# Inverses of chunks one and two in rounds of two batches, with the early parts and the first feed-forward steps dealt out anew

## The chip, the cores and the metric

The kernel runs on one core of one Trainium2 chip. The metric is the device time of one execution in microseconds (us). Every input lies in HBM before the launch, and the output is written back to HBM.

## What is computed

The reference is a recurrent attention block (RWKV-7) followed by a feed-forward block (FFN) with a squared ReLU, all in float32:

```python
# batch 4, heads 8, sequence 768, head size 40; state starts at zero
for t in range(S):
    y[:, :, t] = einsum('bhd,bhde->bhe', rt, state)
    Sa = einsum('bhde,bhe->bhd', state, at)
    state = state * wt[:, :, None, :] - einsum('bhd,bhe->bhde', Sa, bt)
    state = state + einsum('bhd,bhe->bhde', vt, kt)
# y as tokens: 3072 x 320
h = maximum(x @ w_in, 0)        # 320 -> 2048
out = (h * h) @ w_out           # 2048 -> 320
```

## The kernel before

The sequence is cut into six chunks of 128 positions. An **item** is one chunk of one batch; there are 24 items, numbered so that item `i` is chunk `i // 4` of batch `i % 4` (`order`, line 126). Inside a chunk the recurrence is solved with matrix products, for which the inverse of two triangular 64x64 blocks for each head is needed. The work of one item has these parts:

- `early(i)` (line 308, driven by `prepare`, line 623, which first loads the inputs of item `i + 1`): transposes of w, b and a on TensorE, cumulative products and reciprocals on VectorE, 16 products that give the triangular blocks `N`, a copy of them by ScalarE, and stores to HBM: the decays (`kept_e`), the triangular blocks (`kept_d`) and the block between the halves (`kept_n`). Stores are put into a list (`line`, line 86) and issued on SP's queue one or two ticks later; `flush` issues all that are left.
- `solve(u)` (line 360): one **round** of inverses, for a unit `u` of several items, on GpSimd (POOL). It loads the triangular blocks of the whole unit into `half_n`, clears `half_t`, and then goes through the 63 rows of a 64x64 block; for each row one multiplication (line 385) and one subtraction (line 387). Each block lies on several partitions, each of which holds a part of its columns: column `j` lies on class `j` modulo the number of classes. At the end the result is stored to `kept_t`.
- `rest(i)` (line 438): the part of an item that needs no state: it loads `dec` from `kept_e`, multiplies k and v and masks the products. It ends in `inverses(i)` (line 394), which loads `T` from `kept_t` on SP's queue. For the first item of a unit this load stands at the end of `rest`, for the others earlier.
- `chain(i)` (line 500): the part that needs the state and `T`. It is a chain of small products and copies, and gives the tokens of the item.
- the FFN (`ffn`, line 571): for each group of two items 16 steps that multiply by `w_in`, and then 8 steps that multiply by `w_out`, so 24 FFN steps for each of 12 groups. It starts on a group when both of its items are done.

A main loop (line 693) runs 24 steps. Step `i` runs `chain(i)`, `rest(i + 1)`, the early parts of some later items (`ahead`), a number of FFN steps (`share`; otherwise 12), and in steps 0 to 3 the rounding of the weights. `weave` (line 611) deals them out over 12 ticks, in program order for each engine. Each engine and each DMA queue works off its instructions in this order; an instruction that waits holds up what stands behind it on the same engine. SP's queue issues nearly all loads and stores; POOL's queue issues those of `solve`.

Units (line 272): chunk 0 is solved in two units of two batches with a finer scheme (`fine`), each of the chunks 1 to 5 in one unit of four batches, with each block's columns on two partitions (4 batches x 8 heads x 2 halves x 2 classes = 128 partitions). A unit of four items is solved after the step in which the early part of its fourth item is done: chunk 1 after step 1, chunk 2 after step 4, chunks 3 to 5 after steps 7, 11 and 15. Ahead of step 4 a stretch of its own runs 32 FFN steps together with the early parts of items 10 and 11 (`between`, line 686). No early part runs after step 15. After step 23 the rest of the FFN runs alone.

```python
        if u >= FINE:
            for col in range(2):
                queue.dma_start(out=T[col::2], in_=kept[col].rearrange("h f j t -> (f j) h t"))
```

Of the kernel before, what the change touches and what calls it, by code (L numbers as in the profile page):

```python
# [8 lines left out]
FP32 = mybir.dt.float32  # L9
# [8 lines left out]
def kernel(  # L18
# [22 lines left out]
    nc = tc.nc  # L41
# [64 lines left out]
    class Ring:  # L106
# [133 lines left out]
    def weights(n, pool=ps_f):  # L240
        for _ in range(n):
# [8 lines left out]
            else:  # L250
# [15 lines left out]
              for c in range(NCH)]  # L266
# [2 lines left out]
    kept_q = dram.tile([B, H, 2, 2, Q, Q], FP32, tag="q", name="kept_q")  # L269
    kept_m = [dram.tile([2, Q, H, Q], FP32, tag=f"m{i}", name=f"kept_m{i}") for i in range(B)]  # L270

    units = [(0, b0, 2) for b0 in range(0, B, 2)] + [(c, 0, B) for c in range(1, NCH)]
    FINE = B // 2
    unit_of = {c * B + b0 + n: u for u, (c, b0, nb) in enumerate(units) for n in range(nb)}
    kept_t = [dram.tile([2, nb, H, 2, 2, Q // 2, Q] if u < FINE else [2, nb, H, 2, Q, HC], FP32, tag=f"t{u}",
                        name=f"kept_t{u}") for u, (_, _, nb) in enumerate(units)]

    def turn(x_):
        p_ = psum(ps_w)
# [80 lines left out]
    def solve(u, queues):  # L360
        c, b0, nb = units[u]
        fine = u < FINE
        size = Q if fine else HC
        words = lambda t_, n: t_.rearrange("p s t -> p (s t)")[:, :n]
        if fine:
            parts = [words(new(f"half_n{u}", [128, Q, HC - u * Q], 1), Q * Q)]
            kept = [kept_q[b0:b0 + nb].rearrange("b h f k s t -> (b h f k) (s t)")]
            ts = words(solved, Q * HC)[:, u * Q * Q // 2:(u + 1) * Q * Q // 2]
        else:

            parts = [words(new(f"half_n{n}", [128, Q, HC - n * Q], 1), Q * (HC - n * Q)) for n in range(2)]
            kept = [k_.rearrange("b h f s t -> (b h f) (s t)") for k_ in kept_d[c]]
            ts = words(solved, Q * HC)
        for part, from_ in zip(parts, kept):
            for col in range(2):
                queues[col % len(queues)].dma_start(out=part[col * 64:(col + 1) * 64], in_=from_)  # L376
        nc.gpsimd.memset(ts, 0.0)
        for col in range(2):
            nc.gpsimd.memset(ts[col * 64:(col + 1) * 64, col::size + 2], -1.0)
        t3 = ts.rearrange("p (j t) -> p j t", t=size)  # L380
        for s in range(size - 1):
            n, m_ = s // 2 + 1, size - 1 - s
            row = parts[s // Q].rearrange("p (s t) -> p s t", s=Q)[:, s % Q, s % Q + 1:]
            p_ = new("half_p", [128, 528], 1)[:, :n * m_].rearrange("p (j t) -> p j t", j=n)
            nc.gpsimd.tensor_tensor(p_, row.unsqueeze(1).to_broadcast([128, n, m_]),  # L385
                                    t3[:, :n, s:s + 1].to_broadcast([128, n, m_]), Alu.mult)
            nc.gpsimd.tensor_tensor(t3[:, :n, s + 1:], t3[:, :n, s + 1:], p_, Alu.subtract)  # L387
        to = kept_t[u]
        to = to.rearrange("two b h f k j t -> (two b h f k) (j t)") if fine else to.rearrange("two b h f j t -> (two b h f) (j t)")
        nc.gpsimd.dma_start(out=to, in_=ts)  # L390
# [3 lines left out]
    def inverses(i, g, queue=nc.sync):  # L394
        bb, c = order[i]
        u = unit_of[i]
        kept = kept_t[u][:, bb - units[u][1]]
        g["T"] = T = new("T", [128, H, HC], 2)
        if u >= FINE:
            for col in range(2):  # L400
                queue.dma_start(out=T[col::2], in_=kept[col].rearrange("h f j t -> (f j) h t"))
        else:


            blocks = spare("blocks", i)
            for col in range(2):
                queue.dma_start(out=blocks[col::2], in_=kept[col].rearrange("h f k j t -> (f k j) h t"))
        if "N" not in g:
            g["N"] = new("N21", [HC, H, HC], 2)
            queue.dma_start(out=g["N"], in_=kept_n[i])  # L410
            if u < FINE:
                g["joins"] = spare("joins", i)
                for half in range(2):
# [209 lines left out]
    def prepare(i, g=None):  # L623
        if i + 1 < len(order) and i + 1 not in early_loaded:
            load_early(i + 1)
        yield from early(i, g)

    def some(gen, n):
        for _ in range(n):
            next(gen, None)  # L630
            yield
# [50 lines left out]


    TOTAL = STEPS // GB
    ahead = {0: (4, 5), 1: (6, 7), 2: (8,), 3: (9,)}
    between = {4: (10, 11)}
    ahead.update({i: (i + 8,) for i in range(4, len(order) - 8)})
    share = {0: (0, 0), 1: (0, 0), 2: (6, 0), 3: (6, 0), 4: (2, 32), 5: (2, 0)}
    rounded = {0: NARROW - WITH, 1: 5, 2: 5, 3: 6}
    rounding = weights(NARROW + NF)  # L690
    done = set(range(B))
    turn_of = B
    for i in range(len(order)):
        bb, c = order[i]
        n, before = share.get(i, (TOTAL, 0))
        if before:
            made = between.get(i, ())
            jobs = [(some(second, before), before, 0, before)]
            jobs += [(prepare(m_), 5, 8 * j, 8 * j + 10) for j, m_ in enumerate(made)]
            weave(*jobs)  # L700
            done.update(made)
        tc.no_sync_barrier()
        jobs = [(chain(i, ready.pop(i)), 9, 0, TOTAL)]
        if 1 < i + 1 < len(order):
# [8 lines left out]
        if i in rounded:  # L713
            jobs.append((some(rounding, rounded[i]), rounded[i], 0, TOTAL))
        weave(*jobs)
        if turn_of < len(order) and all(turn_of + n_ in done for n_ in range(B)):
            flush()
            solve(unit_of[turn_of], own)
            turn_of += B
    flush()  # L720
    run(second)
    flush()
# [29 lines left out]
```

## Time and profile before

| | us |
|---|---|
| median of 3 runs | 1226.81 |
| lowest and highest of them | 1225.35 and 1228.97 |
| the profiled execution | 1221.21 |
| span of the profiled execution, first to last instruction | 1219.5 |
| TensorE matmul busy | 1035.6 |
| VectorE busy | 491.8 |
| ScalarE busy | 243.5 |
| GpSimd busy | 623.5 |
| mean granted clock of TensorE | 0.878 |

The profile is one execution on the chip. Its page gives the busy time of each engine, the span in 40 slices of 30.5 us, the chain of work that ended last and the costliest groups of instructions. Of its trace one can ask for windows (the busy time of each engine in a stretch), the timeline of one engine, and groups of instructions by shape. In such rows `PE` is TensorE's products, `PEld` its weight loads, `DVE` VectorE, `ACT` ScalarE, `POOL` GpSimd; an engine's name with `q` is its queue or sequencer, so `SPq` shows the issues of DMAs by SP. Times are counted from the span's start. A bracket at the end of a timeline row is the idle time of the engine just before, and what ended it.

### The profile page before, as it was taken

Reading aid. Unit: us, or ns where it says so; the run is one execution under the profiler, and the core shown is the slowest. Engines: PE = TensorE matmul, PEld = TensorE weight load, DVE = VectorE, ACT = ScalarE, POOL = GpSimd, SP = SyncE. Lnnn points to the kernel's source line nnn. Section 1 sums busy time; section 2 is a strip of 40 time slices with the busy share of each in tenths; the row PEclk is TensorE's granted clock in tenths of the full one; section 3 lists DMA queues with packets and bytes.
Section 4 is the critical chain, followed back from the end, with each engine's and each line's share of the span. In section 5 each row is a group of like instructions: output and inputs, shape, how many; then the busy total and the mean of one; then the engine's idle time right before and its main releaser. Section 6 shows DMA issues by size and latency. Waiting matters only on the chain.

```text
span 1219.5 us, 18757 instructions
## 1 busy us (share of the span) xinstructions
PE 1035.6 (85%) x7504; PEld 857.1 (70%) x7504; DVE 491.8 (40%) x1012; ACT 243.5 (20%) x539; POOL 623.5 (51%) x846
## 2 busy tenths in 40 slices
PE   4347677787298989987999978999989999999998
PEld 3336566676177777776878766888768787888876
DVE  5384663566033245424335415435413242322311
ACT  1123212231021112121212121222122121221211
POOL 5670003999517998029996039995059993000000
PEclk9655565788689789997998997999989999999999
DMA  7954468260275643472553381554173113433000
GB/s 97 175 128 104 94 134 164 93 122 37 66 146 99 116 78 77 110 141 72 93 124 81 69 155 53 95 121 107 47 143 63 34 48 84 81 63 74 2 13 11
DMA packets 260822, 110.23 MB, mean 90 GB/s; under 512 B 242944, under 2 KB 248064, under 8 KB 259456
## 3 DMA queue, kind: packets, MB, share of 16 engines
q1 hardware_dynamic: 251824, 83.87, 35.4%
q0 software_dynamic: 2640, 14.16, 4.4%
q10 hardware_dynamic: 6272, 11.01, 3.3%
q8 instruction: 59, 0.97, 0.3%
q14 instruction: 27, 0.22, 0.1%
HBM read 73.28 MB, written 34.74 MB: 89 GB/s over the span
## 4 chain that ended last, share of the span: by engine, by line
PE 60%; POOL 9%; DVE 7%; DMA 5%; SPq 3%; issue 1%; ACT 0%; DVEq 0%; ACTq 0%; POOLq 0%
PE ps_f L77 34%; PE ps_c L77 16%; PE ps_w L77 6%; POOL half_t L387 5%; POOL half_p L385 4%; DMA dec<-kept_e 3%; PE ps_w L281 2%; SPq L132 2%; DVE decay L322 1%; DVE decay L323 1%; PE ps_w L478 1%; DVE RV L297 1%; PE ps_c L488 1%; SPq L98 1%; DMA half_n<-kept_d 1%
## 5 line engine op out<-in xcount | busy, mean ns | idle before, releaser
L387 POOL TENSOR_TENSOR half_t<-half_t,half_p 128x62 f32<-128x62 f32 (+26 forms) x377 | 305.6, 811 | 29.5
L385 POOL TENSOR_TENSOR half_p<-half_n,half_t 128x62 f32<-128x62 f32 (+26 forms) x377 | 277.2, 735 | 74.8 <-DMA half_n<-kept_d 29.1
L77 PE MATMUL ps_f<-tokens,w_in 128*128 128x256 f32 x1152 | 300.5, 406 | 6.6 <-DVE w_out L236 5.3
L77 PEld LDWEIGHTS ps_f<-tokens,w_in 128*128 128x128 f32 x1152 | 219.2, 200 | 40.7 <-DVE w_out L236 5.6
L77 PE MATMUL ps_f<-w_out,hid 128*128 128x320 f32 x768 | 227.6, 445 | 0.0
L583 DVE TENSOR_TENSOR hid<-ps_f,hid 128x256 f32<-128x256 f32 x192 | 80.6, 420 | 341.2 <-ACT hid L582 341.2
L77 PEld LDWEIGHTS ps_f<-w_out,hid 128*128 128x128 f32 x768 | 142.8, 193 | 54.6 <-issue 3.1
L376 POOL DMA_DIRECT2D half_n<-kept_d x20 | 10.2, 518 | 282.7 <-DMA kept_d<-N 282.5
L582 ACT ACTIVATE hid<-ps_f 128x256 f32<-128x256 f32 x192 | 73.6, 383 | 311.1 <-PE ps_f L77 311.1
L77 PE MATMUL ps_w<-dec,kvT 40*128 40x128 f32 x384 | 35.4, 333 | 40.5 <-DVE kvT L454 36.2
L77 PEld LDWEIGHTS ps_c<-xr,T 64*64 64x64 f32 x768 | 52.7, 145 | 19.1 <-issue 15.2
L77 PEld LDWEIGHTS ps_w<-dec,kvT 40*128 40x128 f32 x384 | 30.0, 231 | 46.0 <-DVE kvT L454 38.4
L77 PE MATMUL ps_c<-xr,T 64*64 64x40 f32 x768 | 58.5, 237 | 2.1 <-ACT xr L513 2.1
L77 PE MATMUL ps_w<-rT,xnT 40*128 40x128 f32 x384 | 36.3, 311 | 21.1 <-DVE RV L297 20.2
L77 PEld LDWEIGHTS ps_c<-in_v,A 128*128 128x128 f32 x384 | 51.2, 209 | 1.6 <-issue 0.2
L77 PEld LDWEIGHTS ps_w<-rT,xnT 40*128 40x128 f32 x384 | 29.8, 208 | 31.4 <-DVE RV L297 26.0
L77 PE MATMUL ps_c<-in_v,A 128*128 128x40 f32 x384 | 50.3, 294 | 0.0
L297 DVE TENSOR_TENSOR A<-ps_w,upper 128x512 f32<-128x512 f32 x48 | 30.9, 685 | 47.5 <-PE ps_w L77 47.5
L281 PE MATMUL ps_w<-ident,in_w 128*128 128x128 f32 x96 | 20.2, 347 | 34.5 <-DMA in_w<-in_w_dram 34.4
L334 ACT COPY N<-ps_w 128x512 f32<-128x512 f32 x48 | 25.8, 589 | 115.4 <-PE ps_w L77 66.4
L318 DVE TENSOR_TENSOR_SCAN decay<-ps_w,ones 128x64 f32<-128x64 f32 x88 | 23.6, 268 | 60.8 <-PE ps_w L281 60.8
L77 PE MATMUL ps_w<-decay,bT 40*128 40x128 f32 x352 | 29.9, 318 | 18.8 <-DVE decay L327 18.8
(123 smaller groups left out, 1284.2 us busy)
## 6 DMA issues: line engine op xcount, KB each, us to landing
kept_e<-decay SPq DMA_DIRECT2D x22, 780.0 KB
dec<-kept_e SPq DMA_DIRECT2D x22, 780.0 KB
half_n<-kept_d POOLq DMA_DIRECT2D x10, 512.0 KB, 8.0
kept_t<-half_t POOLq DMA_DIRECT2D x5, 1024.0 KB, 4.2
T<-kept_t SPq DMA_DIRECT2D x40, 128.0 KB
in_w<-in_w_dram SPq DMA_DIRECT2D x24, 160.0 KB
in_ab<-in_b_dram SPq DMA_DIRECT2D x24, 160.0 KB
in_ab<-in_a_dram SPq DMA_DIRECT2D x24, 160.0 KB
```

What stands on the lines that cost most here:

```text
L77: nc.tensor.matmul(o, l_, r_, start=start, stop=True, skip_group_check=True)
L98: later(lambda: queue.dma_start(out=out_, in_=in_), steps)
L132: nc.sync.dma_start(out=t_[:, :, :D], in_=src[bb, :, c * C:(c + 1) * C, :].rearrange("h t d -> t h d"))
L281: nc.tensor.transpose(p_[:, q * 128:(q + 1) * 128], pair(x_, q), ident)
L297: nc.vector.tensor_tensor(t_, p_, over4(upper), Alu.mult)
L318: nc.vector.tensor_tensor_scan(up[:, q, MID + 1:C + 1], wT[:, q, MID:], ones, 1.0, Alu.mult, Alu.mult)
L322: nc.vector.reciprocal(down[:, :, MID + 1:C + 1], up[:, :, MID + 1:C + 1])
L334: nc.scalar.copy(t_[:, e * NP:(e + 1) * NP], p_)
L385: nc.gpsimd.tensor_tensor(p_, row.unsqueeze(1).to_broadcast([128, n, m_]), t3[:, :n, s:s + 1].to_broadcast([128, n, m_]), Alu.mult)
L387: nc.gpsimd.tensor_tensor(t3[:, :n, s + 1:], t3[:, :n, s + 1:], p_, Alu.subtract)
L582: nc.scalar.activation(h_, p_, Act.Relu)
L583: nc.vector.tensor_tensor(h_, p_, h_, Alu.mult)
```

## The change

Four things change together.

1. **Units.** Chunks 1 and 2 are also solved in units of two batches. Units 2 and 3 are chunk 1, units 4 and 5 are chunk 2; chunks 3, 4 and 5 keep one unit of four.
2. **Columns on four partitions.** A unit of two batches has 2 x 8 x 2 = 32 blocks, and each block's columns lie on four partitions. The blocks are loaded four times instead of twice, 32 partitions each. For row `s` there are `s // 4 + 1` columns on a partition instead of `s // 2 + 1`. `half_t` holds two such units in turn, in its first and its second 1024 words. `T` is read in four DMAs with every fourth partition instead of two with every second.
3. **Early parts.** The early parts of items 4 to 15 run in steps 0 to 7, in the numbers 2, 1, 1, 1, 2, 1, 2, 2 (before: 2, 2, 1, 1, two in the stretch ahead of step 4, then 1, 1, 1, 1). A unit is solved after the step in which its last item is done: units 2 to 5 after steps 0, 2, 4 and 5, chunk 3 after step 7 as before. Chunks 4 and 5 stay as they were. Each solve is preceded by `flush`.
4. **FFN steps.** Ahead of step 4 there are 4 FFN steps instead of 32, and steps 4 and 5 have 12 each instead of 2. All later steps keep 12.

```diff
-    units = [(0, b0, 2) for b0 in range(0, B, 2)] + [(c, 0, B) for c in range(1, NCH)]
+    units = [(c, b0, 2) for c in range(3) for b0 in range(0, B, 2)] + [(c, 0, B) for c in range(3, NCH)]
...
+    classes = lambda u: 2 if u < FINE else 128 // (units[u][2] * 2 * H)
+    kept_t = [dram.tile([2, nb, H, 2, 2, Q // 2, Q] if u < FINE else [classes(u), nb, H, 2, HC // classes(u), HC], FP32,
+                        tag=f"t{u}", name=f"kept_t{u}") for u, (_, _, nb) in enumerate(units)]
...
+        cols = classes(u)
+        rows = 128 // cols
...
-            kept = [k_.rearrange("b h f s t -> (b h f) (s t)") for k_ in kept_d[c]]
-            ts = words(solved, Q * HC)
+            kept = [k_[b0:b0 + nb].rearrange("b h f s t -> (b h f) (s t)") for k_ in kept_d[c]]
+            size_of = HC // cols * HC
+            at = u % 2 * size_of if cols > 2 else 0
+            ts = words(solved, Q * HC)[:, at:at + size_of]
         for part, from_ in zip(parts, kept):
-            for col in range(2):
-                queues[col % len(queues)].dma_start(out=part[col * 64:(col + 1) * 64], in_=from_)
+            for col in range(cols):
+                queues[col % len(queues)].dma_start(out=part[col * rows:(col + 1) * rows], in_=from_)
         nc.gpsimd.memset(ts, 0.0)
-        for col in range(2):
-            nc.gpsimd.memset(ts[col * 64:(col + 1) * 64, col::size + 2], -1.0)
+        for col in range(cols):
+            nc.gpsimd.memset(ts[col * rows:(col + 1) * rows, col::size + cols], -1.0)
         t3 = ts.rearrange("p (j t) -> p j t", t=size)
         for s in range(size - 1):
-            n, m_ = s // 2 + 1, size - 1 - s
+            n, m_ = s // cols + 1, size - 1 - s
...
-            for col in range(2):
-                queue.dma_start(out=T[col::2], in_=kept[col].rearrange("h f j t -> (f j) h t"))
+            for col in range(classes(u)):
+                queue.dma_start(out=T[col::classes(u)], in_=kept[col].rearrange("h f j t -> (f j) h t"))
...
-    ahead = {0: (4, 5), 1: (6, 7), 2: (8,), 3: (9,)}
-    between = {4: (10, 11)}
-    ahead.update({i: (i + 8,) for i in range(4, len(order) - 8)})
-    share = {0: (0, 0), 1: (0, 0), 2: (6, 0), 3: (6, 0), 4: (2, 32), 5: (2, 0)}
+    ahead = {0: (4, 5), 1: (6,), 2: (7,), 3: (8,), 4: (9, 10), 5: (11,), 6: (12, 13), 7: (14, 15)}
+    ahead.update({i: (i + 8,) for i in range(8, len(order) - 8)})
+    share = {0: (0, 0), 1: (0, 0), 2: (6, 0), 3: (6, 0), 4: (TOTAL, 4)}
...
-        if before:
-            made = between.get(i, ())
-            jobs = [(some(second, before), before, 0, before)]
-            jobs += [(prepare(m_), 5, 8 * j, 8 * j + 10) for j, m_ in enumerate(made)]
-            weave(*jobs)
-            done.update(made)
+        for _ in range(before):
+            next(second)
+            tick()
...
-        if turn_of < len(order) and all(turn_of + n_ in done for n_ in range(B)):
+        while unit < len(units) and all(m_ in done for m_ in range(len(order)) if unit_of[m_] == unit):
             flush()
-            solve(unit_of[turn_of], own)
-            turn_of += B
+            solve(unit, own)
+            unit += 1
```

More of the change, by code (lines that the diff above doesn't have):

```diff
@@ L270 @@
     kept_m = [dram.tile([2, Q, H, Q], FP32, tag=f"m{i}", name=f"kept_m{i}") for i in range(B)]
-    units = [(0, b0, 2) for b0 in range(0, B, 2)] + [(c, 0, B) for c in range(1, NCH)]
+    units = [(c, b0, 2) for c in range(3) for b0 in range(0, B, 2)] + [(c, 0, B) for c in range(3, NCH)]
     FINE = B // 2
     unit_of = {c * B + b0 + n: u for u, (c, b0, nb) in enumerate(units) for n in range(nb)}
-    kept_t = [dram.tile([2, nb, H, 2, 2, Q // 2, Q] if u < FINE else [2, nb, H, 2, Q, HC], FP32, tag=f"t{u}",
-                        name=f"kept_t{u}") for u, (_, _, nb) in enumerate(units)]
+    classes = lambda u: 2 if u < FINE else 128 // (units[u][2] * 2 * H)
+    kept_t = [dram.tile([2, nb, H, 2, 2, Q // 2, Q] if u < FINE else [classes(u), nb, H, 2, HC // classes(u), HC], FP32,
+                        tag=f"t{u}", name=f"kept_t{u}") for u, (_, _, nb) in enumerate(units)]
     def turn(x_):
@@ L691 @@
     done = set(range(B))
-    turn_of = B
+    unit = FINE
     for i in range(len(order)):
```

## The prediction, made before the changed kernel was run

> **What bounds the kernel now.** I read the page first: the slices, then the shares of the chain that ended last.
>
> ```profile
> span 1219.5 us, 18757 instructions
> PE   4347677787298989987999978999989999999998
> POOL 5670003999517998029996039995059993000000
> PEclk9655565788689789997998997999989999999999
> PE 60%; POOL 9%; DVE 7%; DMA 5%; SPq 3%; issue 1%; ACT 0%; DVEq 0%; ACTq 0%; POOLq 0%
> ```
>
> TensorE is full in the second half; its holes lie in the first third and at slices 10, 18, 24 and 30. POOL holds 9% of the chain, although it idles in between. So I cut the trace into steps, from the first product of one chain to that of the next (step 3 ends where the 32 FFN steps begin, at 291).
>
> ```profile
> 141.50:197.40 55.90, 37.05 (x302) 33.75 (x300) 32.26 (x68) 13.59 (x29) 1.25 (x3) 0.59 0.68 156
> 197.40:245.90 48.50, 41.22 (x302) 34.37 (x301) 23.07 (x49) 12.13 (x29) 38.50 (x53) 0.67 0.58 120
> 245.90:291.00 45.10, 34.66 (x252) 28.58 (x250) 30.17 (x65) 12.21 (x28) 42.20 (x38) 0.77 0.50 106
> 291.00:376.86 85.86, 61.68 (x282) 48.22 (x279) 22.08 (x49) 12.12 (x29) 39.42 (x64) 0.84 0.42 89
> 376.86:409.50 32.64, 27.89 (x249) 24.22 (x248) 15.33 (x29) 5.42 (x11) 30.05 (x34) 0.90 0.34 83
> 409.50:449.20 39.70, 33.90 (x250) 28.25 (x250) 15.57 (x29) 5.52 (x11) 37.11 (x34) 0.79 0.51 94
> 449.20:487.60 38.40, 36.32 (x303) 31.19 (x301) 19.01 (x41) 9.60 (x22) 34.87 (x46) 1.00 0.49 96
> 487.60:531.00 43.40, 42.62 (x319) 34.00 (x318) 15.15 (x33) 7.38 (x16) 0.90 (x3) 1.00 0.45 108
> 531.00:583.00 52.00, 41.07 (x303) 35.07 (x301) 19.10 (x41) 9.60 (x22) 40.57 (x55) 0.87 0.52 103
> 711.30:764.35 53.05, 41.18 (x304) 35.25 (x302) 19.85 (x41) 9.60 (x22) 41.38 (x56) 0.84 0.53 101
> 889.70:931.80 42.10, 36.35 (x275) 31.46 (x274) 13.08 (x29) 8.53 (x21) 31.29 (x47) 0.88 0.47 93
> 971.70:1004.80 33.10, 33.10 (x276) 28.77 (x274) 14.60 (x29) 8.52 (x20) 30.75 (x31) 1.00 0.26 57
> 1044.80:1076.10 31.30, 31.30 (x258) 26.92 (x258) 11.88 (x27) 8.53 (x20) 0.00 (x0) 1.00 0.42 80
> 1076.10:1114.40 38.30, 38.30 (x276) 30.10 (x274) 8.62 (x19) 6.30 (x14) 0.00 (x0) 1.00 0.39 65
> ```
>
> The columns are window, length, busy time of PE, PEld, DVE, ACT and POOL (instructions), granted clock, DMA share, GB/s. The rows are steps 1, 2, 3, the stretch ahead of step 4, steps 4 to 8, 12, 16, 18, 20 and 21. From step 6 on TensorE sets the pace (36.32 of 38.40). Not in the stretch: 61.68 of 85.86, though it has FFN work in hand. Steps 4 and 5 have only two FFN steps each, and wait and run at 0.90 and 0.79.
>
> ```profile
> 336.30 1.09 PE L281 MATMUL ps_w<-ident,in_w 128*128 128x128 f32 x4 [23.16 <-DMA in_w<-in_w_dram]
> 291.77 2.78 SPq L98 DMA_DIRECT2D tokens<-tokens  x4
> 327.98 1.34 SPq L401 DMA_DIRECT2D T<-kept_t  x2
> 332.82 0.57 SPq L132 DMA_DIRECT2D in_w<-in_w_dram  x1
> 323.76 0.60 POOL L390 DMA_DIRECT2D kept_t<-half_t  x1 [0.30 <-POOL half_t L387]
> ```
>
> Here is why. POOL stores chunk 1's inverses at 323.76. SP's queue stands from 294.55 to 327.98 at the load of `T`, and item 11's inputs are behind it. TensorE meets their transposes and idles 23.16 us with FFN products queued behind.
>
> **The change part by part.** The sum is made against the profiled execution (span 1219.5, time 1221.2), which is 5.6 below the median shown; I apply the difference to that median.
>
> *Price of a round.*
>
> ```profile
> L387 POOL TENSOR_TENSOR half_t<-half_t,half_p 128x528 f32<-128x528 f32 x5 | 6.0, 1209 | 0.4
> L385 POOL TENSOR_TENSOR half_p<-half_n,half_t 128x528 f32<-128x528 f32 x5 | 5.5, 1101 | 0.4
> L387 POOL TENSOR_TENSOR half_t<-half_t,half_p 128x62 f32<-128x62 f32 x10 | 3.1, 306 | 0.8
> L385 POOL TENSOR_TENSOR half_p<-half_n,half_t 128x62 f32<-128x62 f32 x10 | 2.9, 289 | 0.8
> 196.15 1.53 POOL L376 DMA_DIRECT2D half_n<-kept_d  x3 [100.82 <-DMA kept_d<-N]
> 206.62 0.28 POOL L385 TENSOR_TENSOR half_p<-half_n,half_t 128x63 f32<-128x63 f32 x1 [6.04 <-DMA half_n<-kept_d]
> 707.50 1.34 SPq L401 DMA_DIRECT2D T<-kept_t  x2
> ```
>
> From 62 to 528 elements the pair grows from 595 to 2310 ns: 3.68 ns an element, 367 ns fixed, and 80 ns of gap behind each instruction, 527 ns a row in all. Two classes have the sum of (s//2+1)(63-s) = 22352 elements over 63 rows: 33.2 + 82.3 = 115.5 us, measured 323.76 - 206.62 = 117.1. Four classes have 11696: 33.2 + 43.0, scaled alike 77 us; half the width isn't half the time. Loading takes 206.62 - 196.15 = 10.5; four more issues at 0.51 make 12.5. A round of two items is 90 us, of four 128. Twos cost POOL 52 us more per chunk, but the first pair is there early. By my step times below, round 2 runs 142-232, needed near 287; round 3 242-332, needed near 397; round 4 346-436, needed at the end of step 7; round 5 436-526, at the end of step 9; round 6 (chunk 3) 526-654, and with 4.2 to land (323.76 to 327.98) and about 3 to read, 661. It is needed by chain(12), before at 711.3 (T issued at 707.50), after near 670. All fit, the last one narrowly. The two more loads of `T` per item (1.34/2 = 0.67 each on SP) lie beside full TensorE time.
>
> The Trainium skill (DMA: Bandwidth & Descriptors, Anatomy of one DMA) gives a POOL-issued DMA about 2.0 us fixed, mostly its write receipt. Paid one after another, eight loads would take some 8 us more than four, 16 us later over rounds 4 and 5: `T` at 677, 7 late, and 1207 for the sum. Against it, the four issues here overlap: all landed 10.5 us after the first. This is the late-round rival.
>
> *Steps 0 to 3.* One early part leaves step 1 (55.9, against 48.5 in step 2, which has one early part and six FFN steps besides): -7. The load of round 2 moves from the start of step 2 to that of step 1; round 3 brings a new one to step 3: +3, between 0 and a full collision. Sum **-4**.
>
> *The stretch and steps 4 to 7.*
>
> ```profile
> 449.20:487.60 38.40, 17.88 (x73) 12.80 (x72) 4.97 (x12) 4.60 (x12) 1.00 0.49 96
> 487.60:531.00 43.40, 24.81 (x89) 15.84 (x88) 1.70 (x4) 2.38 (x6) 1.00 0.45 108
> ```
>
> These are the FFN's own shares (the instructions on `ps_f`; PE, PEld, DVE, ACT) of steps 6 and 7. A `w_in` step costs 17.88/12 = 1.49, a `w_out` step (24.81 - 4 x 1.49)/8 = 2.36. Step 6 has twelve of the first, step 7 four of the first and eight of the second. After the change 40 FFN steps instead of 48 are done by the end of step 5, so the kinds change places: even steps hold eight `w_out` and four `w_in`, odd steps twelve `w_in`. An early part costs 38.40 - 31.30 = 7.1 or 43.40 - 38.30 = 5.1; I take 6.
>
> A collision is the new wait:
>
> ```profile
> 533.28 2.03 POOL L376 DMA_DIRECT2D half_n<-kept_d  x4 [44.41 <-DMA kept_d<-N]
> 548.18 1.04 SPq L445 DMA_DIRECT2D dec<-kept_e  x1
> 554.27 2.08 PE L77 MATMUL ps_w<-dec,kvT 40*128 40x128 f32 x16 [9.07 <-DVE kvT L454]
> 425.61 1.16 PE L77 MATMUL ps_w<-dec,kvT 40*128 40x128 f32 x16 [1.16 <-DVE kvT L454]
> ```
>
> After a solve, `flush` puts the stores ahead of the next loads on SP, and `half_n` takes the DMA engines meanwhile; `dec` goes out at 548.18, and TensorE stands 9.07 us and then runs at half speed (2.08 for products that take 1.16 in step 5). Step 8 is 52.0 against 38.4, step 12 53.05, step 16 42.1 against 33.1 in step 18: 9 to 14.6. It hits step 5 in full (round 4 starts at once): 12. After step 5 POOL is still busy with round 4, so round 5's load falls into the middle of a step: I take 4 in step 6 for the flush, between 0 and 13.6.
>
> So: four `w_in` steps 6.0; step 4, 43.4 + 6 + 4 (clock, which was 0.77 in step 3) = 53.4; step 5, 38.4 + 12 = 50.4; step 6, 43.4 + 6 + 4 = 53.4; step 7, 38.4 + 6 = 44.4. Sum 207.6, against 85.86 + 32.64 + 39.70 + 38.40 + 43.40 = 240.0: **-32.4**.
>
> On the clock the Trainium skill (TensorE: Matmul & The Clock Gate, What you observe ff.) says that an idle window of some 3.4 us halves the rate until as long a busy one ends. The half-speed row behind the 9.07 us agrees. By that rule step 4, without the 23 us hole, would soon be warm and my 4 near 0: 1196.
>
> *Step 8* loses its collision in part, since round 6 begins near 526, inside the step and not at its start: **-5** (0 to -13.6). *Steps 12 and 16* now have four `w_out` steps (9.4) instead of four `w_in` (6.0) ahead of the waiting product: **-4** (0 to -7). *Tail:* eight `w_out` steps come after the loop: 8 x 2.36 = **+18.9**, with nothing beside them.
>
> Sum: -4 - 32.4 - 5 - 4 + 18.9 = -26.5, so 1226.8 - 26.5 = **1200**.
>
> **The rivals.**
>
> - *Late rounds.* For it: chunk 3's round waits behind two others, and the slack at chain(12) is 670 - 661 = 9 us. Twenty us of delay cost 11: 1211, up to 1221 where they are 30. Against it: POOL's prices are regular.
> - *Slower: a full collision after each flush.* One mechanism: the loads of `dec` behind stores and `half_n`. In full (13.6) in steps 1, 3, 5, 6 and 8, with step 2 freed of the 3.4 by which it exceeds step 3, it gives -7 + 13.6 + 13.6 - 3.4 = +17; then 6 + 53.4 + 52 + 63 + 44.4 - 240 = -21; then 0, 0, +18.9: +15, or 1241. Two full collisions beyond the one that I count use up the 26.5; a third decides it. For it: steps 8, 12, 16. Against: step 2 shows hardly any, and POOL delays two of the loads.
> - *Nothing left.* Two early parts in a step cost more than 12: in step 1 they went with 18.8 us of idle TensorE. With 8 more in each of steps 4, 6 and 7: 1224. Against: there, FFN products stand in between.
> - *More:* no collision in steps 5 and 6 and none left in step 8: another 16 to 25 less, which chain(12)'s slack of 9 cuts to 9: 1191, or to 1184 where the rounds begin sooner too.
>
> **How the numbers follow.** The forecast (1192 to 1208) has 0.50, late rounds 0.18, more 0.10, nothing left 0.12, slower 0.10. A measurement tells about 0.3% (3.7 us) from no change. Faster: the forecast, "more", nearly all of "late rounds", and a quarter of "nothing left", 0.80; same 0.09; slower 0.11. The range runs from "more" to "nothing left", 1184 to 1224; outside it are the collisions and a little at the low end.
>
> **What would show it.** The 23.16 us wait gone; the start of chain(8) near 495 instead of 531; solves of 90 us back to back from round 4; chain(12) near 670 with no wait on `T`; waits of `kvT` for `dec` in step 5 and less in step 8; a tail longer by 19. I am wrong if TensorE waits for `T` in step 12, or if steps 1, 3, 6 show gaps like that at 554.

## The result, and the profile after

| | before | after |
|---|---|---|
| median of the runs of this comparison, us | 1226.08 (1223.73 to 1228.97) | 1178.59 (1174.56 to 1181.60) |
| profiled execution, us | 1221.21 | 1178.52 |
| its span, us | 1219.5 | 1176.8 |

The ratio is 0.961, with a 95% interval of 0.9574 to 0.9645: 3.9% faster, 47.5 us by the medians, 42.7 by the spans. The forecast was 26.5 less and 1200; the time lies below the range's low end of 1184.

These are the lines of the page after the change that answer to those shown of before:

```profile
span 1176.8 us, 19057 instructions
PE   4436646887899999998999979999999999999998
POOL 5761068827887887878999399980399970000000
PEclk9999996576899999998999989999999999999999
PE 38%; DVE 2%; DMA 2%; SPq 2%; issue 0%; ACT 0%; DVEq 0%; ACTq 0%
```

The hole of slice 10 is gone (slices are counted from 0). POOL works almost without a break from slice 6 to slice 21, but for slice 8, where round 3 waits for the blocks of item 7. It no longer stands in the chain that ended last (that chain was followed back over less of the span than before: its shares add up to 42%, before to 85%). One line needs care: the granted clock reads 9 in the first six slices, where before it read 5 or 6 in all but the first. The products there are no faster: the 16 products that open chain(0) take 3.63 us in both traces.

The same cut into steps (columns as before: window, length, PE, PEld, DVE, ACT, POOL, clock, DMA share, GB/s). The rows are steps 1, 2, 3, the FFN steps ahead of step 4, steps 4 to 8, step 12, and step 23 with the tail:

```profile
141.70:203.70 62.00, 34.57 (x274) 30.95 (x273) 26.75 (x56) 12.52 (x27) 42.87 (x82) 0.87 0.66 141
203.70:256.00 52.30, 45.18 (x310) 38.05 (x310) 23.45 (x49) 13.20 (x31) 29.98 (x59) 0.63 0.42 91
256.00:309.50 53.50, 39.57 (x254) 33.27 (x253) 30.86 (x68) 12.73 (x29) 39.83 (x77) 0.71 0.55 118
309.50:316.10 6.60, 6.60 (x31) 5.33 (x29) 2.01 (x5) 1.54 (x4) 5.91 (x9) 1.00 0.31 75
316.10:361.00 44.90, 43.91 (x344) 35.80 (x343) 21.19 (x45) 8.47 (x18) 36.34 (x79) 1.00 0.81 168
361.00:402.00 41.00, 38.68 (x305) 32.76 (x303) 18.87 (x41) 9.62 (x22) 36.24 (x61) 0.96 0.45 81
402.00:446.85 44.85, 43.86 (x344) 35.75 (x342) 21.13 (x45) 8.46 (x18) 36.14 (x77) 1.00 0.84 162
446.85:486.90 40.05, 38.92 (x331) 33.48 (x330) 24.72 (x53) 10.69 (x24) 35.31 (x61) 1.00 0.60 120
486.90:529.50 42.60, 41.82 (x317) 33.64 (x315) 15.61 (x33) 7.39 (x16) 34.47 (x66) 1.00 0.68 147
658.40:711.20 52.80, 45.45 (x315) 35.96 (x314) 17.29 (x33) 7.40 (x16) 37.93 (x53) 0.90 0.54 112
1092.10:1176.80 84.70, 80.72 (x423) 64.26 (x421) 13.87 (x31) 14.73 (x37) 0.00 (x0) 1.00 0.03 9
```

Set against the prediction's terms, in us:

| part | before | after | change | predicted |
|---|---|---|---|---|
| steps 0 to 3, from 95.6 / 95.4 to the FFN steps ahead of step 4 | 195.4 | 214.1 | +18.7 | -4 |
| FFN steps ahead of step 4, and steps 4 to 7 | 240.0 | 177.4 | -62.6 | -32.4 |
| step 8 | 52.0 | 42.6 | -9.4 | -5 |
| steps 9 to 11 | 128.3 | 128.9 | +0.6 | 0 |
| steps 12 to 22 | 434.4 | 433.7 | -0.7 | |
| step 23 and tail | 73.8 | 84.7 | +10.9 | |
| the last two together | 508.2 | 518.4 | +10.2 | -4 + 18.9 |

So two terms were far off, in opposite directions. The first steps got slower where they should have got a little faster, and the stretch with steps 4 to 7 gained nearly twice what was forecast. Of the +18.7, step 0 has 0.4, step 1 6.1, step 2 2.4 and step 3 9.9. (The prediction's row for step 2 ends at 245.90, but the first product of chain(3) starts at 247.36; with that edge steps 2 and 3 were 50.0 and 43.6 before.)

Where the forecast put a full collision, into step 5, there is almost none. POOL's timeline after the change, and one row of SP's, show why (start, length, engine, operation; the bracket is the idle time ahead and what ended it):

```profile
259.70 3.88 POOL L382 DMA_DIRECT2D half_n<-kept_d  x8 [21.25 <-DMA kept_d<-N]
347.70 0.60 POOL L396 DMA_DIRECT2D kept_t<-half_t  x1 [0.30 <-POOL half_t L393]
348.30 3.88 POOL L382 DMA_DIRECT2D half_n<-kept_d  x8
356.94 0.29 POOL L391 TENSOR_TENSOR half_p<-half_n,half_t 128x63 f32<-128x63 f32 x1 [3.15 <-issue]
650.62 0.60 POOL L396 DMA_DIRECT2D kept_t<-half_t  x1 [0.30 <-POOL half_t L393]
656.64 1.35 SPq L407 DMA_DIRECT2D T<-kept_t  x2
```

Round 4 is written in the program behind step 4 (316 to 361), but its load goes out at 348, inside the step, and POOL works on it at 357, before step 5 begins. POOL knows no steps: it waits only for round 3 (done at 347.70) and for the blocks of items 8 and 9. Those were there already, since the row of the load has no idle time ahead of it: item 9's early part is the first of the two in step 4. Chunk 3's round ended at 650.62, and the load of T(12) went out at 656.64 without a wait in the products behind it: the late rounds did not come, and the estimate of 654 for that end was near. So was the price of a round: round 2's rows ran from 160.83 to 237.84, 77.0 us, and from the first issue of its load (148.83) it took 89.0, where 77 and 90 were forecast. Its eight loads were not paid one after another: all had landed 12.0 us after the first issue.

And step 1, which lost an early part and grew from 55.9 to 62.0. Rows of four timelines of the kernel after:

```profile
154.01 7.96 SPq L132 DMA_DIRECT2D in_ab<-in_a_dram  x1
162.97 0.50 DVE L227 TENSOR_SCALAR ps_f<-w_out 128x320 int32<-128x320 int32 x1 [7.68 <-DMA w_out<-in_moe_w_out_dram]
163.50 0.50 ACT L229 ACTIVATE ps_f<-ps_f,lowest 128x320 int32<-128x320 int32 x1 [9.35 <-DVE ps_f L227]
165.10 1.09 PE L537 MATMUL ps_c<-ident,minus_x 128*128 128x128 f32 x4 [8.51 <-ACT minus_x L533]
170.79 2.08 PE L77 MATMUL ps_w<-dec,kvT 40*128 40x128 f32 x16 [4.60 <-DVE kvT L460]
```

Round 2's load was issued from 148.83 to 152.88. SP then needs 7.96 us to issue one load. VectorE waits 7.68 us for a piece of `w_out`; ScalarE stands 9.35 us at the next step of that rounding; the chain's copy is behind it on ScalarE, and TensorE waits 8.51 us for the copy. That is a second road for a collision, which the prediction did not have: through the weight loads and the rounding into the chain.

### The profile page after: what moved, and what is told of

It is laid out like the page before. It is cut to its first block, busy times and chain, and to the rows that moved or that the text cites. A ratio compares the mean times of both kernels' runs of the same rounds, so it can differ in the third digit from the quotient of the medians.

```text
span 1176.8 us, 19057 instructions
## 1 busy us (share of the span) xinstructions
PE 1026.8 (87%) x7504; PEld 849.5 (72%) x7504; DVE 491.0 (42%) x1012; ACT 243.9 (21%) x539; POOL 692.7 (59%) x1138
## 5 line engine op out<-in xcount | busy, mean ns | idle before, releaser
L391 POOL TENSOR_TENSOR half_p<-half_n,half_t 128x252 f32<-128x252 f32 (+51 forms) x503 | 304.8, 606 | 88.5 <-DMA half_n<-kept_d 30.5
L393 POOL TENSOR_TENSOR half_t<-half_t,half_p 128x252 f32<-128x252 f32 (+51 forms) x503 | 332.9, 662 | 39.4
L588 ACT ACTIVATE hid<-ps_f 128x256 f32<-128x256 f32 x192 | 73.8, 384 | 316.4 <-PE ps_f L77 316.4
L382 POOL DMA_DIRECT2D half_n<-kept_d x44 | 21.6, 500 | 132.2 <-DMA kept_d<-N 78.0
L460 DVE TENSOR_TENSOR kvT<-ps_w,dec 128x512 f32<-128x512 f32 x24 | 16.5, 688 | 129.8 <-DMA dec<-kept_e 81.9
L77 PEld LDWEIGHTS ps_c<-xr,T 64*64 64x64 f32 x768 | 52.8, 145 | 22.0 <-issue 17.4
L299 DVE TENSOR_TENSOR A<-ps_w,upper 128x512 f32<-128x512 f32 x48 | 30.9, 685 | 47.6 <-PE ps_w L77 47.5
```

The lines of the kernel that those rows point to most:

```text
L77: nc.tensor.matmul(o, l_, r_, start=start, stop=True, skip_group_check=True)
L299: nc.vector.tensor_tensor(t_, p_, over4(upper), Alu.mult)
L382: queues[col % len(queues)].dma_start(out=part[col * rows:(col + 1) * rows], in_=from_)
L460: nc.vector.tensor_tensor(kT, kT_, down[:, :, 1:C + 1], Alu.mult)
L588: nc.scalar.activation(h_, p_, Act.Relu)
```

## The experiments

Ratios are to runs of the kernel before on the same chip, with 95% intervals; the changed kernel stands at 0.961. Step lengths are from the first product of one chain to the first of the next, so that step 3 holds the FFN steps ahead of step 4 (before 129.5, after 60.1). Each is from one execution, and in the first steps that matters: up to the end of step 2, `load_at_edge`, `double_load`, `no_lag` and `ffn_ahead_of_step4` are the same program as the changed kernel, and their step 2 took 51.1, 46.8, 46.8 and 47.1, where that of the changed kernel took 52.3 and that of the kernel before 50.0. Their step 1 took 60.9 to 62.7.

### The two halves of the change

`twos_old_dealing`: the new rounds with the early parts and FFN steps dealt as before.

```diff
-    ahead = {0: (4, 5), 1: (6,), 2: (7,), 3: (8,), 4: (9, 10), 5: (11,), 6: (12, 13), 7: (14, 15)}
+    ahead = {0: (4, 5), 1: (6, 7), 2: (8,), 3: (9,)}
+    between = {4: (10, 11)}
...
-    share = {0: (0, 0), 1: (0, 0), 2: (6, 0), 3: (6, 0), 4: (TOTAL, 4)}
+    share = {0: (0, 0), 1: (0, 0), 2: (6, 0), 3: (6, 0), 4: (2, 32), 5: (2, 0)}
```

> Rounds of two items for chunks 1 and 2 as in the changed kernel, but the early parts and the FFN steps dealt as before (32 FFN steps ahead of step 4, two each in steps 4 and 5). Theory A, that the gain has two halves (the 23 us hole that the earlier round closes, and FFN products beside the chain in steps 4 and 5): the hole goes, steps 4 and 5 stay at 33 to 40 us, 1195 to 1208 in all. Rival B, that the hole alone makes the gain: within 5 us of the changed kernel, 1174 to 1184.

Measured: 1218.09, ratio 0.991 (0.9886 to 0.9933). A smaller gain than either theory said. The same kernel once more:

> The kernel of twos_old_dealing once more, for an undisturbed profile. Rounds in twos alone close the hole (step 3 and the stretch 104 instead of 129.5) but bring step 1 from 56 to 63 or more; the whole again 1212 to 1220. If steps 4 to 6 are no longer than 33, 40 and 39 now, the growth seen there came from the disturbed run.

Measured: 1219.92, ratio 0.9918 (0.9889 to 0.9948). Step 3 with the stretch is 104.2, so the hole is closed (-25.3). But step 1 is 64.7 (+8.8), step 4 36.8 (+4.5) and step 6 45.8 (+7.4). The earlier rounds alone give back most of what the hole was worth; why steps 4 and 6 grew is not shown.

`fours_new_dealing`: the new dealing with rounds of four for chunks 1 and 2.

```diff
-    units = [(c, b0, 2) for c in range(3) for b0 in range(0, B, 2)] + [(c, 0, B) for c in range(3, NCH)]
+    units = [(c, b0, 2) for c in range(1) for b0 in range(0, B, 2)] + [(c, 0, B) for c in range(1, NCH)]
```

> The new dealing with rounds of four items on two classes for chunks 1 and 2. Theory A: chunk 1's round can begin only after step 2, near 260, and needs 128 us, while T(4) is wanted near 311; TensorE waits some 70 to 80 us ahead of chain(4), 1240 to 1265 in all. Rival, that the dealing is the gain and the rounds in twos do little: below 1190.

Measured: 1290.18, ratio 1.0501 (1.0459 to 1.0544). The wait in step 4 is as large as expected, but there is a second one, in step 8 (95.2 us long), for chunk 2, which the expectation left out. TensorE's timeline, in step 4 and in step 8:

```profile
385.86 1.90 PE L77 MATMUL ps_c<-xr,T 64*64 64x40 f32 x16 [74.19 <-DMA T<-kept_t]
604.75 1.90 PE L77 MATMUL ps_c<-xr,T 64*64 64x40 f32 x16 [40.60 <-DMA T<-kept_t]
```

So the dealing needs the rounds in twos: with fours it is worse than before, and the early pair is what makes it possible.

`ffn_ahead_of_step4`: all of the change but the FFN steps, 32 of which stay ahead of step 4, with two each in steps 4 and 5 (the same `share` line as above).

> The changed kernel with before's FFN shares: 32 FFN steps ahead of step 4, two each in steps 4 and 5. Theory A, that FFN products hide the chain's waits: the stretch is 58 us and steps 4 and 5 stay near 37 each, 133 instead of 92.5, and the tail is 12 to 19 shorter: 1195 to 1208. Rival: TensorE's work is only moved, 1174 to 1184.

Measured: 1206.24, ratio 0.982 (0.979 to 0.985). As theory A said: steps 4 and 5 are 33.6 and 37.5 with two FFN steps each, 44.9 and 41.0 with twelve. Ten FFN steps more cost 11.3 and 3.5 us there. From 0.982 to 0.961 is what the FFN steps beside the chain are worth, some 25 us.

`no_lag`: twelve FFN steps ahead of step 4 instead of four.

```diff
-    share = {0: (0, 0), 1: (0, 0), 2: (6, 0), 3: (6, 0), 4: (TOTAL, 4)}
+    share = {0: (0, 0), 1: (0, 0), 2: (6, 0), 3: (6, 0), 4: (TOTAL, 12)}
```

> Twelve FFN steps ahead of step 4 instead of four, so that no FFN steps are behind at the end of step 5. Where TensorE sets the pace from step 4 on, the eight w_out steps only move: the stretch grows from 6.6 to 19 to 26, step 23 with the tail falls from 84.7 to 72 to 75, the whole stays within 5 us of the changed kernel. Rival, that FFN work after the loop is dearer or cheaper than ahead of step 4: a difference of 6 us or more.

Measured: 1185.81, ratio 0.9662 (0.9624 to 0.9699). Step 3 grew by 15.0 to 75.1, step 23 with the tail came down by 10.3 to 74.4. The interval overlaps that of the changed kernel, but by the ratios the difference is 6 us, so this does not decide between the two theories: that the eight steps only move is not shown.

### What a round's load costs, and where

`load_at_edge`: item 10's early part goes from step 4 to step 5, so that item 9's ends with step 4.

```diff
-4: (9, 10), 5: (11,),
+4: (9,), 5: (10, 11),
```

> The early part of item 9 alone in step 4, those of 10 and 11 in step 5. Item 9's blocks are then stored at the end of step 4, so that round 4's load falls on the edge between steps 4 and 5. Theory A, that step 5 escaped the collision only because round 4's load began at 348, inside step 4: step 5 grows from 41 to 49 to 54, and the whole by 5 to 12 (1184 to 1191). Rival, that a collision costs little where TensorE has FFN products: step 5 below 45, within 3 us of the changed kernel.

Measured: 1188.95, ratio 0.9688 (0.9647 to 0.9728); step 5 is 51.0, and step 7 grows too, from 40.1 to 50.4 (round 5's load is at 448 here, beside that step's start at 453). In POOL's and TensorE's timelines round 4's load now stands at the edge (step 5 begins at 357), and the wait of `kvT` for `dec` is there:

```profile
359.46 3.88 POOL L382 DMA_DIRECT2D half_n<-kept_d  x8 [11.54 <-DMA kept_d<-N]
379.68 2.08 PE L77 MATMUL ps_w<-dec,kvT 40*128 40x128 f32 x16 [6.98 <-DVE kvT L460]
```

In the changed kernel that wait is 0.64 us:

```profile
375.96 1.16 PE L77 MATMUL ps_w<-dec,kvT 40*128 40x128 f32 x16 [0.64 <-DVE kvT L460]
```

Theory A holds: step 5 escaped because of where the load fell. The step also has one early part more here, worth some 2.4 us by the next run, so some 7.6 of the 10.0 us are the load's.

`step1_two_early`: item 7's early part back in step 1, those of 8 to 10 each a step earlier.

```diff
-1: (6,), 2: (7,), 3: (8,), 4: (9, 10), 5: (11,),
+1: (6, 7), 2: (8,), 3: (9,), 4: (10,), 5: (11,),
```

> Item 7's early part goes back to step 1, item 8's to step 2, 9's to step 3, 10's to step 4, one each in steps 4 and 5. The prediction priced the early part that leaves step 1 at 7 us. If that is right, step 1 grows from 62 to about 69 and steps 2 and 3 stay. Rival, that step 1 is set by the weights' loads and the chain: step 1 stays within 3 us of 62, and step 3 falls by 4 to 8, since round 3's load then begins when round 2 ends, inside step 2.

Measured: 1158.95, ratio 0.9426 (0.9394 to 0.9457), clearly faster than the changed kernel. Step 1 is 64.5: the early part is worth 2.5 us there, not 7. Step 4, with one early part fewer, is 42.5 instead of 44.9: 2.4, not 6. Step 3 is 52.7 instead of 60.1: round 3's load now goes out at 238, when round 2 ends, inside step 2. Step 9 falls from 46.7 to 41.3, since chunk 3's load is 21 us earlier too (501 instead of 522).

`no_rounding_step1`: no roundings in step 1, eight each in steps 2 and 3.

```diff
-    rounded = {0: NARROW - WITH, 1: 5, 2: 5, 3: 6}
+    rounded = {0: NARROW - WITH, 1: 0, 2: 8, 3: 8}
```

> No rounding of weights in step 1; steps 2 and 3 do eight pieces each instead of five and six. Theory D, that step 1 is slow since the half_n load holds up a weight load, VectorE's rounding waits for it, ScalarE's copy of the chain waits behind the rounding and TensorE behind that copy: step 1 falls from 62 to 48 to 53, steps 2 and 3 grow by 2 to 5 each. Rival, that it is the load of dec (4.6 us of wait) and the chain alone: step 1 stays above 57.

Measured: 1180.45, ratio 0.9609 (0.9572 to 0.9646). Step 1 is 56.2, between the two theories, and steps 2 and 3 grow by about 8 each, with three and two roundings more. The rounding is one road into the chain and not the whole cost; this did not settle it. The next run did.

`round2_later`: POOL waits for the transposes of chain(1) before it loads round 2 (it clears padding that is zero already, and must wait until TensorE has read it).

```diff
+    def gated(u):
+        nc.gpsimd.memset(pads(minus_x.tiles[1]), 0.0)
+        solve(u, own)
+        yield
...
+        if i == 1:
+            jobs.append((gated(FINE), 1, 7, 8))
...
             flush()
-            solve(unit, own)
+            if unit > FINE:
+                solve(unit, own)
```

> The changed kernel, but GpSimd first waits for the transposes of chain(1) (by a clearing of padding that holds zeros already) and then loads round 2, near 160 instead of 149. Theory E, that step 1 is slow since that load meets the step's first loads and the weight loads: step 1 falls from 62 to 52 to 57. Rival, that the load costs the same wherever it falls in a step without FFN products: 60 to 64. The later rounds move by some 10 us, which steps 1 to 11 can take; step 12 may wait for T.

Measured: 1169.45, ratio 0.9536 (0.952 to 0.9553). Step 1 falls from 62.0 to 53.0. Round 2's load starts 11 us later. SP's two loads that took 3.01 and 7.96 us to issue take 1.14 each, VectorE's wait for the piece of `w_out`, 7.68 in the changed kernel, is 0.87, and TensorE's wait for the chain's copy, 8.51, is 1.71. Rows of four timelines:

```profile
151.92 1.14 SPq L132 DMA_DIRECT2D in_ab<-in_a_dram  x1
155.97 0.49 DVE L227 TENSOR_SCALAR ps_f<-w_out 128x320 int32<-128x320 int32 x1 [0.87 <-DMA w_out<-in_moe_w_out_dram]
158.10 1.09 PE L537 MATMUL ps_c<-ident,minus_x 128*128 128x128 f32 x4 [1.71 <-ACT minus_x L533]
159.84 1.96 POOL L382 DMA_DIRECT2D half_n<-kept_d  x4 [0.32 <-issue]
```

Nothing but the time of the load, and of POOL's work behind it, was moved, and the waits that went are waits for DMAs and what hung on them. So theory E is shown: the load at the step's start costs step 1 some 9 us.

`no_flush`: the solve is put into the list of stores, behind those that it needs, instead of a flush at the step's end.

```diff
-            flush()
-            solve(unit, own)
+            later(lambda u=unit: solve(u, own), 3)
             unit += 1
```

> The changed kernel without the flush at the end of a step with a solve: the stores go out in their turn, behind the next step's first loads, and the solve stands behind them. Theory C1, that the slow steps 1, 3, 9, 12 and 16 come from the traffic of the half_n load: no change, 1174 to 1184. Theory C2, that they come from the order on SP's queue (stores ahead of loads): each loses some 4 to 8 us, 1145 to 1162.

Measured: 1172.71, ratio 0.9558 (0.9521 to 0.9595), an interval that overlaps that of the changed kernel. Steps 1 (61.2) and 12 (51.4) stay slow without the flush, and step 16 falls by 3.9. Step 2 is 47.1, but three of the kernels named above, which keep the flush, have 46.8 to 47.1. The order on SP's queue is at most a small part.

`double_load`: each load of chunks 4 and 5 made twice.

```diff
             for col in range(cols):
-                queues[col % len(queues)].dma_start(out=part[col * rows:(col + 1) * rows], in_=from_)
+                for _ in range(2 if c > 3 else 1):
+                    queues[col % len(queues)].dma_start(out=part[col * rows:(col + 1) * rows], in_=from_)
```

> The changed kernel with each half_n load of chunks 4 and 5 made twice (the second over the first). Theory C1, that a collision is the traffic of that load beside the next item's loads: steps 12 (52.8) and 16 (43.0) grow by 3 to 10 each, the whole by 5 to 20. Theory C2, that it is the order on SP's queue or the copy of the blocks: steps 12 and 16 within 2 us, the whole within 4.

Measured: 1184.35, ratio 0.9661 (0.9615 to 0.9706); step 12 is 52.8 as in the changed kernel and step 16 is 39.1. Step 20 grew from 37.4 to 48.1, with a wait of 7.79 us for `T`: chunk 5's round was late by the longer load. Inconclusive: the second load of a tile waited for the first to land, so the traffic was drawn out over 32 us instead of doubled. It does not tell the theories apart.

### Moving the loads

`tick7_only`: the changed kernel, with a step's first or only early part run in its first 7 ticks of 12.

```diff
-            jobs.append((prepare(m_), 5, j * 5, TOTAL - 5 * (len(made) - 1 - j)))
+            jobs.append((prepare(m_), 5, j * 5, j * 5 + 7))
```

> The changed kernel with the first early part of each step run in its first 7 ticks. Theory A (a load costs by where it falls): steps 5, 9, 11, 13 and 16 fall by 3 to 8 each, the whole by 15 to 35, to 1145 to 1165. Rival, that early_by_tick7 owes its time to the other order of the early parts in steps 1 to 4: above 1168.

Measured: 1139.91, ratio 0.9293 (0.9274 to 0.9312), more than expected. Steps 5, 9 and 16 fall by 4.9, 5.5 and 3.9; round 3's load, now at 238, leaves step 3 (53.2). But steps 11, 13 and 15 fall too, by 2.6, 4.3 and 3.6, and no load of a round stands at their start. So the theory covers only a part. Step 12, the other way, grew to 57.8, with a wait of 11.4 us for `T`. Step 15 in windows, first of the changed kernel:

```profile
795.30:835.00 39.70, 38.84 (x304) 32.90 (x303) 18.06 (x41) 9.62 (x22) 0.00 (x0) 0.96 0.37 77
```

and of `tick7_only`:

```profile
766.00:802.00 36.00, 36.00 (x303) 31.19 (x302) 18.14 (x41) 9.61 (x22) 9.18 (x20) 1.00 0.53 119
```

The work is the same, but the clock is not. Inside that step TensorE's timeline of the changed kernel has

```profile
819.79 1.75 PE L77 MATMUL ps_w<-rT,xnT 40*128 40x128 f32 x16 [0.18 <-DVE RV L299]
822.12 0.89 PE L484 MATMUL ps_w<-ident,dec 128*128 128x128 f32 x4 [0.58 <-DVE RX L299]
822.79 2.77 PE L77 MATMUL ps_f<-tokens,w_in 128*128 128x256 f32 x6
```

where `tick7_only` has no wait and six such products in half the time:

```profile
797.18 2.76 PE L77 MATMUL ps_f<-tokens,w_in 128*128 128x256 f32 x12
```

Small waits, and then products at half speed. With the early part's products spread otherwise the waits are gone. But the half speed in step 15 belongs to this one execution: in `step1_two_early` and `round2_later` the same two waits (0.18 and 0.58) are followed by

```profile
805.09 1.46 PE L77 MATMUL ps_f<-tokens,w_in 128*128 128x256 f32 x6
```

(that row is of `step1_two_early`), and step 15 takes 38.0 in both. So the waits are worth 1.9 of the 3.6 us, and 1.7 came with the half speed. In step 13, where the first of the two waits is about 2 us, the half speed came back in all three kernels; the changed kernel has

```profile
737.53 1.75 PE L77 MATMUL ps_w<-rT,xnT 40*128 40x128 f32 x16 [2.02 <-DVE RV L299]
739.86 0.66 PE L484 MATMUL ps_w<-ident,dec 128*128 128x128 f32 x4 [0.58 <-DVE RX L299]
740.36 2.64 PE L77 MATMUL ps_f<-tokens,w_in 128*128 128x256 f32 x6
```

`early_by_tick7`: this and the order of `step1_two_early` together.

> Early parts as in step1_two_early, and a step's only or first early part is run in its first 7 ticks of 12, so that its blocks are stored, and a waiting round loaded, before the step's end. Theory A, that what a load costs depends on where it falls: steps 12 and 16 lose 4 to 10 each (50 and 44 before), 1139 to 1152. Rival, that the load's traffic costs the same anywhere: within 4 us of step1_two_early, 1153 to 1163.

Measured: 1132.71, ratio 0.9222 (0.9195 to 0.9248). Step 16 loses 4.7 against `step1_two_early` (39.1), but step 12 is 54.2, and now, as in `tick7_only`, for another reason. TensorE's timeline there:

```profile
640.32 1.90 PE L77 MATMUL ps_c<-xr,T 64*64 64x40 f32 x16 [10.57 <-DMA T<-kept_t]
```

That is the late-round rival, which came true once everything ahead of it was faster.

`early_by_tick7_no_flush` (its edit is that of `no_flush`):

> The same without the flush at the end of a step with a solve. Theory: what no_flush gained (about 6 us of the changed kernel) came from steps 2 and 16, and part of it is gone once the stores are out before the step ends: 0 to 6 us less than early_by_tick7. Rival, that the two gains add: 6 or more.

Measured: 1138.23, ratio 0.9264 (0.9237 to 0.9291): no gain, if anything a loss.

`chunk3_twos`: `early_by_tick7` with chunk 3 in two rounds as well (`range(3)` becomes `range(4)` in the line of units).

> early_by_tick7 with chunk 3 in rounds of two as well. Theory F, that step 12's 54 us there is a wait for T(12), as the 10.6 us row of TensorE says, and that chunk 4's load falls at the same edge: T(12) comes some 40 us earlier, the load near 670, step 12 falls to 41 to 46 and the whole to 1116 to 1127. Rival, that step 12's time is only the collision: 1128 to 1137.

Measured: 1155.80, ratio 0.942 (0.9402 to 0.9438), a miss. Step 12 fell to 41.3, as theory F said. But two rounds take POOL some 175 us (500 to 675) where one takes 127 (501 to 629 in `step1_two_early`), and the next one is late: step 16 is 56.2, with a wait of 14.5 us for `T`, and two loads now fall at the edges of steps 11 and 13 (45.1 and 46.8). With `round2_later` on top:

> chunk3_twos and round2_later together. If theory E holds, 5 to 10 us less than chunk3_twos; by the rival the same within 4.

Measured: 1169.23, ratio 0.9529 (0.9506 to 0.9551). Step 1 gains 7.5 again, but every later round is some 13 us later, and the loads meet the edges of steps 5 and 7 (42.1 and 47.5). What is right for step 1 is wrong for the rounds behind it.

`early_by_tick7_fill`: `early_by_tick7` with eight FFN steps more ahead of step 12.

```diff
-    share = {0: (0, 0), 1: (0, 0), 2: (6, 0), 3: (6, 0), 4: (TOTAL, 4)}
+    share = {0: (0, 0), 1: (0, 0), 2: (6, 0), 3: (6, 0), 4: (TOTAL, 4), 12: (TOTAL, 8)}
```

> early_by_tick7 with eight FFN steps more ahead of step 12, which then are missing from the tail. If step 12's 54 us hold an idle wait of 10.6 us for T(12), these 18.9 us of products fill it: steps 11 and 12 together grow by 8 to 10 instead of 19, the tail falls by 11 to 19, 1119 to 1129 in all. Rival, that FFN steps only move (as in no_lag): 1130 to 1138.

Measured: 1122.71, ratio 0.9147 (0.9123 to 0.9172), the fastest kernel of the study. Steps 11 and 12 together even fall, from 90.3 to 88.7, with eight FFN steps more in them; no product waits for `T` any more, and the tail is shorter.

## Why the prediction was wrong

The mechanism was right: the earlier pair closes the hole, FFN steps fill steps 4 and 5, the tail pays for it, and the rounds just fit. Two of its sums were wrong, and one of them in sign; that they went opposite ways hid a part of each in the total.

**"It hits step 5 in full (round 4 starts at once): 12."** This step failed. The round did start at once, but not at the step's edge: POOL started as soon as round 3 was done, 13 us before the edge, since the blocks of items 8 and 9 were there. So step 5 took 41.0, not 50.4. `load_at_edge` put the load at the edge, and step 5 took 51.0, of which some 2.4 are the early part that came with it. The same holds for step 6: I took 4, and it is 44.85, as step 4 without any flush ahead (44.9). The prediction reasoned about POOL in the program's steps; POOL's queue has none.

**"An early part costs 7.1 or 5.1; I take 6."** It costs 2.4 (step 4 in `step1_two_early`) or 2.5 (step 1). One cause is in the prediction's own rows: steps 20 and 21 were taken for steps without an early part, but they belong to chunk 5, whose chain makes no state update, and step 18 has 276 products where step 20 has 258. With steps 18 and 19 (33.1 and 40.0) the price would have been 5.3 or 3.4. The rest hangs on how the early part is spread over its step: in `step1_two_early` step 15 with one takes 38.0 and step 17, with the same FFN steps and none, 34.5; in `tick7_only` they take 36.1 and 34.3. Three steps that got a second one (4, 6 and 7) were so overpriced by 3.6 each.

**The clock's 4 in step 4** was 0: the windows give 1.00 for the FFN steps ahead of it and for step 4, and the durations bear it out (31 products in 6.60 us). The alternative by the clock-gate rule of the Trainium skill (TensorE: Matmul & The Clock Gate, What's actually happening) was the better one here.

Together step 5's 9.4, step 6's 4, three times 3.6 and the clock's 4 are 28 of the 30 us by which the stretch and steps 4 to 7 were misjudged.

**Steps 0 to 3, "-7" and "+3".** The early part that left step 1 was worth 2.5. The load moved to the start of step 1 was counted at nothing, because step 2 had borne it before without visible cost. But the two steps differ: `round2_later` puts the load's place in step 1 at 9 us, through the weight loads, the rounding and ScalarE. The load in step 3 was taken at 3 (round 3's, at 259.70, near that step's start at 256), and step 3 up to the FFN steps grew by 9.9; where the load falls into step 2 instead, step 3 is 7.4 shorter (`step1_two_early`), though item 9's early part stands there for item 8's. Step 2's 2.4 is no effect of the change that these runs show: with the same program it took 46.8 us in `double_load`. There TensorE was busy for 39.8 us at a granted clock of 0.72, in the changed kernel for 45.2 at 0.63.

**Step 8, steps 12 to 22, tail.** Step 8 lost 9.4, but here the lengths mislead: from step 4 on even and odd steps have swapped the kinds of their FFN steps. Steps 18, 20 and 22, which no load touches, grew by 6.0 for it, and steps 17, 19 and 21 fell by 5.9 to 6.0. Against its own kind step 8 lost 15, all of its collision, and step 9, which should have fallen by 6.0, grew by 3.2 to 46.7: chunk 3's load went out at 522, near the start of step 9 at 529. With that load at 501 (`step1_two_early`) step 9 is 41.3. So the collision went on into the next step and got smaller; that the -5 came near the sum over steps 8 to 11 (-8.8) was partly luck, since the swap was not counted there. In step 12 the wait of `kvT` for `dec` did get shorter, 5.74 us where it was 9.25. The eight FFN steps cost 10.2 with steps 12 to 22, against 14.9.

**The rivals.** A collision after every flush did not come: two of the five steps named (1 and 3) had one, and steps 5, 6 and 8 escaped through POOL's own timing; step 9, which it did not name, had one in part. "More" (1184 to 1191) had the direction, and its condition came true: no collision to speak of in steps 5 and 6 and none left in step 8. Its limit, the slack of chain(12), moved with the rounds, which ended at 650.6 instead of 654: `T`(12) went out at 656.6, and chain(12) began at 658.4, so the late rounds only just did not come.

## What to carry to other kernels

Here a load on POOL's queue started when its data and the work ahead of it on that queue were done, not where the program's step ended; to price such a load, find that moment in the trace and see which loads are then under way. When work is moved between steps, take its price from two steps that differ in nothing else: count their instructions first, and ask whether the change swaps the kinds of work between them. And where an early stage becomes faster, ask which round or transfer becomes the next late one; filling its wait with work from the tail was worth more here (1122.71) than making it earlier (1155.80).

## What the runs showed of the hardware

- The granted clock of the trace read 1.00 in step 0 after the change and 0.54 before, while the same 16 products took 3.63 us in both. In the profile after the change it reads 1.00 up to 180 us, where products still take twice their later time (16 of `kvT` 2.08 us at 170.79, 1.16 at 375.96). For that stretch the durations decide, not the column.
- In step 13 waits of 2.02 and 0.58 us were followed by products at half speed (2.64 us for six that otherwise take 1.46), and so in `step1_two_early` (2.05 and 0.58, then 2.77) and `round2_later` (1.90 and 0.58, then 2.69). I had expected this only behind longer waits such as the 9.07. After 0.18 and 0.58 us in step 15 it came in the changed kernel and not in those two.
- While a round's load ran, the issue of one input load by SP took up to 7.96 us; after the first 140 us, those that were not issued within 16 us of such a load took 0.37 to 1.96. With the round's load 11 us later (`round2_later`) the same issue took 1.14. What stands behind it in SP's queue waits with it: the load of `dec` went out at 162.01, there at 153.11.
